# Key copies one group per three steps, the second batch's keys loaded two units later, and two reordered loads in a block-sparse attention plus MoE kernel

## The chip, the core and the metric

The kernel runs on one core of one Trainium2 chip. The metric is device time in microseconds. Three runs of the kernel before gave 733.57 us in the median (733.33 to 733.93).

## What is computed

Block-sparse attention over 4 batches, 8 heads, 768 positions and head size 64, then a two-layer network over all 3072 rows. A block of 32 queries sees the blocks next to it, the first and the last block, and three drawn blocks; the first and the last block of queries see everything.

```python
def reference(q, k, v, sampled_blocks, w_in, w_out):
    scores = (q @ k.transpose(0, 1, 3, 2)) / 8            # 4 x 8 x 768 x 768
    mask = (abs(blk_i - blk_j) <= 1) | edge(blk_i) | edge(blk_j)   # edge: block 0 or 23
    for qb in range(24):
        for kb in sampled_blocks[qb]:                     # three drawn per block of queries
            mask[32*qb:32*qb+32, 32*kb:32*kb+32] = True
    attn = softmax(where(mask, scores, -1e9))
    x = (attn @ v).transpose(0, 2, 1, 3).reshape(3072, 512)
    h = maximum(x @ w_in, 0)                              # w_in 512 x 2048
    return (h * h) @ w_out                                # w_out 2048 x 512
```

## The kernel before, in words

**Tiles and halves.** A tile is 128 positions of one batch, so there are 24, numbered k = 0 to 23 over (batch b, tile t), six to a batch. A tile is worked in two halves u, four heads each (class Half, L423). One half makes the scores on TensorE (L481, tile `s_t_u`), maxima on VectorE (L493), exponentials on ScalarE, a transpose, and the product with the values on TensorE (L576, tile `pv_t_u`). The two whole query blocks of a batch are a unit of their own kind (class Whole, L627, score tile `g`).

**Gathered keys.** The scores of a tile read a buffer KG, in which the keys that each group j of 32 queries needs lie side by side: two fixed blocks, three drawn ones and three neighbours. Two buffers, `KG_84` and `KG_85` in the order tool's names, take turns, and a third serves tile 2 alone. For tiles 0 to 6 GpSimd fills KG out of the batch's natural keys `kn` (one tile for each half, loaded whole by `load_keys`, L185). `copy_keys` (L284) is a generator: for each half it makes the window copies (L317, three instructions) and, for the first tiles of a batch, the fixed blocks (L352), and then for each group j three copies (L299) with a `yield` behind them. So one group per call of `next`. A tile has 4 groups a half, or 3 where an edge block is left out (tiles 0 and 5 of a batch). From tile 7 on KG is loaded by DMA (`load_kg`, L333).

**The network.** Rows go through it in chunks c of three tiles. In chunk 0 the weights are still being prepared: every 128-wide slice f of either layer is loaded as a raw 64-bit tile by a DMA that GpSimd issues (`craw`, L832), cut by ScalarE (L848, L850) and assembled by VectorE (L859, L860) into `W` (first layer) or `WO` (second). A first-layer slice is then split (`split`, L898) into a high part, cast by ScalarE (L901), and a low part, a subtraction on GpSimd (L904); both are the tile `wi_f`. TensorE multiplies three times: high by high, high by low and low by high (L939, tile `ph_f`), so its third matmul of a slice needs GpSimd's subtraction. The second layer is L983 (chunk 0) and L993 (later), tile `po`. The raw tiles and `wi` share one rotating set of seven buffers.

**What sets the order.** Every engine works through its own list in the order in which the code issues instructions; the five lists wait for each other by semaphores. First comes a start phase (L1115 to L1142) with the attention of chunk 0. Then `moe(c)` is a generator whose every `yield` is a step `now` (L1153). In each step of chunk 0 the loop first calls `more_keys` (L328; it advances the oldest unfinished `copy_keys` by one group), then cuts and loads weights, and then lets the units of chunk 1 (tiles 3 to 5) and chunk 2 go on (`work.step`). The halves of tiles 3, 4 and 5 start in steps 4, 16, 28, 40, 52 and 64 (STEP_1 and FIRST_1), those of tile 6, the first of the second batch, in steps 67 and 83. The split of slice f + 1 is issued where slice f begins, about every sixth step.

**Loads of the second batch.** `Half.loads` (L598) with step 0 runs right behind a half's scores. In tile 4 of the first batch (t = NT - 2) it calls `load_keys` for the next batch on GpSimd's DMA queue; in tile 5 it adds the whole blocks' queries and the values `vn`, also there. The drawn rows of values (L396) and the fixed ones (L211, L215) go by SyncE's queue.

**`prepare`** (L1087) runs once, in step 8 of the start phase: the rest of tile 1's keys, its windows of values, drawn rows for tile 1, then for tile 2 (the third tile) the fixed value blocks (`load_static`), the drawn rows and four groups of keys, with one raw-weight load (`advance("load")`) among them.

Of the kernel before, what the change touches and what calls it, by code (L numbers as in the profile page):

```python
# [18 lines left out]
SP = mybir.EngineType.SP  # L19
# [3 lines left out]
B, H, S, D = 4, 8, 768, 64  # L23
# [4 lines left out]
NT = S // P  # L28
NJ = P // BLK
# [52 lines left out]
SOON = 12  # L82
SPLIT_1 = 4
BITS_1 = 5
STEADY = 11
V_3 = (4, 9)

KEYS_0 = 8
# [18 lines left out]
def tile_block_sparse_attention_moe(ctx: ExitStack, tc, kd, knd, qd, qgd, vd, vnd, samp, const, wcat, out):  # L107
# [9 lines left out]
    nc = tc.nc  # L117
# [63 lines left out]
    def load_whole(b, eng=nc.sync):  # L181

        eng.dma_start(QG.rearrange("p a b -> p (a b)"), qgd[b])

    def load_keys(b, u, eng=nc.sync):  # L185

        kn = rot.tile([P, NBLK, 2, BLK], F32, tag=f"kn{u}", name=f"kn{b}_{u}", bufs=1)
        eng.dma_start(kn.rearrange("p a b c -> p (a b c)"), knd[b, u])
        st["kn", b, u] = kn

    def values_of(k):

        return V[k if k < UC else 0]
# [4 lines left out]
    def halves(k, u):  # L198

        if k < UC:  # L200
            return slice(0, 2) if u == k // 2 else None
        return slice(u, u + 1)

    def columns(src, us):

        return src.rearrange("... (u c) -> ... u c", u=2)[..., us, :]

    def load_static(k, u, eng=nc.sync, j=0, n=1):
        if k < UC:
            src = vd[order[k][0], V_STATIC * BLK :].unsqueeze(1).broadcast_to([2 * BLK, n, HW])  # L210
            eng.dma_start(VJ[k][0][0 : 2 * BLK, j : j + n], src)  # L211
            return
        src = columns(vd[order[k][0], V_STATIC * BLK :], u)
        src = src.unsqueeze(1).broadcast_to([2 * BLK, NJ, HW // 2])
        eng.dma_start(values_of(k)[0][0 : 2 * BLK, u], src)  # L215
# [7 lines left out]
    def place(k, j, n):  # L223

        return (j + n - 1 if 0 < k < UC else 1 + n) % NJ
# [19 lines left out]
    def load_vn(b, hf, eng=nc.sync, own=None):  # L245

        vn = (own or rot).tile([P, NT, HW // 2], F32, tag="vn", name=f"vn{b}_{hf}", bufs=1)
        eng.dma_start(vn.rearrange("p t c -> p (t c)"), vnd[b, hf])
        st["vn", b, hf] = vn

    def groups(t):

        return tuple(range(1 if t == 0 else 0, NJ - 1 if t == NT - 1 else NJ))
# [4 lines left out]
    def sampled(t, i, on):  # L258
        n = NJ * NRAND
        a = (2 * t + i) * n  # L260
        return nc.values_load_multi_w_load_instructions(
            st["idx"][0:1, a : a + n],
            engines=[on],
            min_val=0,
            max_val=NBLK - 2,
            skip_runtime_bounds_check_because="products of a block's index with 0 or 1, that is zero unless the index is 1 to 22",
        )[1]

    def load_q(b, t, eng=nc.sync, own=None):
        q = (own or rot).tile([P, NJ, NPAIR, BLK], F32, tag="q", name=f"q{b}_{t}", bufs=1 if own else 2)  # L270
        n = NJ * NPAIR * BLK
        eng.dma_start(q.rearrange("p a b c -> p (a b c)"), qd[b, :, t * n : (t + 1) * n])
        st["q", b, t] = q

    def keys_of(b, t, own=None):

        k = order.index((b, t))
        st["kg", b, t] = own.tile([P, NJ, NK, NPAIR, BLK], F32, name=f"KG{k}") if own else KG[(k - (k >= UC)) % 2]
# [5 lines left out]
    def copy_keys(b, t):  # L284

        vals = sampled(t, 0, POOL)
        k, kg = order.index((b, t)), st["kg", b, t]
        for u in range(2):
            copy = nc.gpsimd.tensor_copy
            if t < UC:  # L290
                static_keys(b, t, u, copy)
            if 0 < k < UC:
                key_edges(k, u, copy)
            else:
                key_windows(k, u, copy)
            kn = st["kn", b, u]
            for j in groups(t):
                for r in range(NRAND):
                    copy(  # L299
                        kg[:, j, key_place(k, j, r), 2 * u : 2 * u + 2].unsqueeze(1),  # L300
                        kn[:, bass.ds(vals[NRAND * j + r], 1)],
                    )
                yield
# [71 lines left out]
    def load_sampled(k, u, eng, on, which=range(NRAND), js=None):  # L375
        us = halves(k, u)
        if us is None:
            return
        b, t = order[k]
        VA, VB = values_of(k)  # L380
        if (b, t) not in drawn:
            drawn.clear()
            drawn[b, t] = sampled(t, 1, on)
        vals = drawn[b, t]
        if k < UC:
            v4 = vd[b].rearrange("(a p) c -> p a c", p=BLK)
        else:
            v4 = columns(vd[b], us).rearrange("(a p) u c -> p a u c", p=BLK)
        for j in sorted(groups(t)) if js is None else js:
            for r in which:  # L390
                a = (place(k, j, 3) if r == 2 else 2 + r) * BLK
                if k < UC:
                    dst = VJ[k][r == 2][a : a + BLK, j]
                else:
                    dst = (VB if r == 2 else VA)[a : a + BLK, us, j]
                eng.dma_start(dst.unsqueeze(1), v4[:, bass.ds(vals[NRAND * j + r], 1)])  # L396
# [26 lines left out]
    class Half:  # L423
# [174 lines left out]
        def loads(self, step):  # L598

            k = order.index((self.b, self.t))  # L600
            eng = nc.gpsimd if self.b == 0 else nc.sync
            if step == 0 and self.t == NT - 2 and self.b + 1 < B:
                load_keys(self.b + 1, self.u, eng)
            if step == 0 and self.t == NT - 1 and self.b + 1 < B:
                if self.u == 0:
                    load_whole(self.b + 1, eng)
                    load_vn(self.b + 1, 0, eng)
            n = k + (UC if k < UC - 1 else UC - 1)
            if step == 0 and self.u == 1 and k != UC - 1 and n < len(order):
                if k < UC:  # L610
                    held.append(order[n])
                else:
                    load_q(*order[n])
                if n <= 2 * UC:
                    keys_of(*order[n])
                    if n < 2 * UC:
                        later.append(copy_keys(*order[n]))
                elif self.moved:
                    load_kg(*order[n])
            if step == 0 and self.u == 0 and k == 2 * UC - 1:  # L620
                later.append(copy_keys(*order[k + 1]))
            if step == 1 and self.u == 1 and 2 * UC < n < len(order):
                load_kg(*order[n])
            if step == 2 and k >= UC and k + 1 < len(order):
                load_values(k + 1, self.u, self.t == NT - 1)
# [251 lines left out]
    def advance(stage):  # L877

        if done[stage] < len(cuts):
            stages[stage](*cuts[done[stage]])  # L880
        done[stage] += 1
# [205 lines left out]
    def prepare():  # L1087
        key_windows(1, 1, nc.gpsimd.tensor_copy)
        deque(keys[1], 0)
        for f in windows(1, 0) + windows(1, 1):  # L1090
            f(nc.gpsimd.tensor_copy)
        load_sampled(1, 0, nc.sync, SP, (2,))
        load_static(2, 1, n=NJ)
        load_sampled(2, 1, nc.sync, SP, (0, 1))
        for j in groups(2):
            next(keys[2])
            if j == 1:
                advance("load")

    def rest(i):  # L1100
        if i == 0:
# [22 lines left out]
    now = 0  # L1124
# [25 lines left out]
    now = 0  # L1150
    for c in range(NCH + 1):
        work.drain(c, now)
        for _ in moe(c):  # L1153
            now += 1
            if c or now > SPLIT_1 and (now < STEADY or now % 2 == 0):
                more_keys()
            if c == 0 and now == SPLIT_1:
                wi1[0, 2] = split(0, W1[2], "wi0_2")
            if c == 0 and now == V_3[0]:
                nc.gpsimd.memset(V[0][1][BLK : BLK + 1, 0, 0, 0:1], 0.0)  # L1160
            if c == 0 and now in V_3:
                load_window(UC, V_3.index(now))
                load_sampled(UC, V_3.index(now), nc.sync, SP)
                if held:
                    load_q(*held.pop())
            if c == 0 and now == BITS_1:
                advance("bits")
            soon = now in CUT_1 or now >= SOON and now % 3 == 0
            if c == 0 and soon and done["split"] < len(cuts):
                cut_next()  # L1170
            if now < begins(c + 1) - LAST:
                work.step(now)
            else:
                work.step(now)
                work.drain(c + 1, now)
# [58 lines left out]
```

## Time and profile before

| | |
|---|---|
| median of three runs | 733.57 us |
| the profiled execution | 734.13 us, of which 732.2 us are its span |
| granted TensorE clock, mean | 0.999 |
| TensorE matmul busy | 707.3 us (97%) |
| GpSimd busy | 555.0 us (76%) |
| VectorE busy | 533.2 us (73%) |
| ScalarE busy | 501.3 us (68%) |

The profile is one execution, with times in us from the span's start. Rows of its timeline give start, length, engine, line, operation, output and input tile and a count, and in square brackets how long the engine had been idle before and what ended the wait. PE is TensorE, PEld its weight loads, DVE VectorE, ACT ScalarE, POOL GpSimd, SP SyncE; a q behind a name is that engine's DMA queue. A row "PE busy (x)" of a table by stretches gives us busy and a count of instructions.

### The profile page before, as it was taken

To read this page: it belongs to the slowest core of one execution; us is meant where nothing else is said; L and a number is where in the kernel's file an instruction comes from. 1 tells how busy PE (TensorE), PEld (TensorE's weight loads), DVE (VectorE), ACT (ScalarE), POOL (GpSimd) and SP (SyncE) were. 2 spreads that over 40 slices of the span, in tenths; PEclk is the share of its full clock that TensorE was granted. 3 is DMA by queue.
4 is the path that set the end of the run, shared out by engine and by line. 5 is a ranking of instruction groups with operands and counts; after the bars stand their busy time and mean duration, and the time that the engine had idled before them with its cause. 6 is when DMAs were issued, how large, how long until landed. Compare 5 with 4: busy or idle time off the path is not lost.

```text
span 732.2 us, 21483 instructions
## 1 busy us (share of the span) xinstructions
PE 707.3 (97%) x7496; PEld 565.7 (77%) x7496; DVE 533.2 (73%) x1056; ACT 501.3 (68%) x1118; POOL 555.0 (76%) x711
## 2 busy tenths in 40 slices
PE   5889999999999999999999999999999999999997
PEld 2666666677788888777878888887778888888996
DVE  5787889687686868678776877768777686647552
ACT  5888787998757856688866875678776767622222
POOL 8979977368766768869786687768877577868985
PEclk9999999999999999999999999999999999999999
DMA  8869999655554565564635556635455352101001
GB/s 272 195 203 289 281 342 238 156 152 135 165 137 113 170 200 145 119 162 112 182 87 139 161 161 188 155 91 150 129 139 148 96 154 51 34 1 44 1 1 43
DMA packets 91934, 105.10 MB, mean 144 GB/s; under 512 B 13715, under 2 KB 77716, under 8 KB 91828
## 3 DMA queue, kind: packets, MB, share of 16 engines
q1 hardware_dynamic: 86020, 81.15, 41.7%
q0 software_dynamic: 5664, 22.45, 9.4%
q8 instruction: 60, 0.98, 0.6%
q14 instruction: 46, 0.38, 0.2%
q10 hardware_dynamic: 144, 0.13, 0.1%
HBM read 97.39 MB, written 6.29 MB: 142 GB/s over the span
## 4 chain that ended last, share of the span: by engine, by line
PE 65%; DVE 12%; ACT 6%; POOL 6%; DMA 4%; issue 3%; SPq 2%; POOLq 0%; DVEq 0%; ACTq 0%
PE ph L939 27%; PE po L993 25%; PE pv L576 5%; PE s L481 5%; DVE m L493 2%; POOL KG L299 2%; PE po L983 1%; DMA craw<-in_w_dram 1%; DVE p L500 1%; DVE pT L531 1%; SPq L396 1%; DVE xl L927 1%; DMA vn<-in_vn_dram 1%; DMA V<-in_v_dram 1%; ACT pm L525 1%
## 5 line engine op out<-in xcount | busy, mean ns | idle before, releaser
L939 PE MATMUL ph<-xh,wi 128*128 128x384 f32 x960 | 275.4, 347 | 0.6 <-POOL wi L904 0.6
L525 ACT ACTIVATE pm<-p 32x256 f32<-32x256 f32 x528 | 219.2, 415 | 15.6 <-DVE p L500 8.4
L993 PE MATMUL po<-wo,gh 128*128 128x512 f32 x672 | 211.7, 396 | 0.0
L904 POOL TENSOR_TENSOR wi<-W,wi 128x512 fp32r<-128x512 f32 x120 | 164.0, 1366 | 56.8 <-DVE wi L903 29.5
L939 PEld LDWEIGHTS ph<-xh,wi 128*128 128x128 f32 x960 | 173.9, 188 | 23.6 <-issue 11.6
L960 ACT ACTIVATE r<-ph 128x384 f32<-128x384 f32 x128 | 62.9, 492 | 170.1 <-PE ph L939 169.4
L904 POOL TENSOR_TENSOR wo<-WO,wo 128x512 fp32r<-128x512 f32 x112 | 144.6, 1291 | 34.1 <-DVE wo L903 32.7
L973 POOL TENSOR_TENSOR gl<-gf,gh 128x384 fp32r<-128x384 f32 x112 | 118.7, 1060 | 64.8 <-DVE gf L971 55.6
L939 PE MATMUL ph<-xl,wi 128*128 128x384 f32 x480 | 161.9, 337 | 0.0
L993 PEld LDWEIGHTS po<-wo,gh 128*128 128x128 f32 x672 | 123.0, 188 | 26.9 <-issue 7.5
L971 DVE SCALAR_TENSOR_TENSOR gf<-ph,r 128x384 f32<-128x384 f32 x112 | 62.0, 554 | 107.5 <-ACT r L960 99.5
L993 PE MATMUL po<-wo,gl 128*128 128x512 f32 x336 | 134.7, 401 | 5.3 <-POOL gl L973 4.9
L939 PEld LDWEIGHTS ph<-xl,wi 128*128 128x128 f32 x480 | 90.2, 188 | 8.9 <-issue 5.2
L903 DVE CAST wo<-WO 128x512 fp32r<-128x512 f32 x112 | 86.3, 770 | 0.0
L993 PEld LDWEIGHTS po<-wo,gl 128*128 128x128 f32 x336 | 63.0, 187 | 25.8 <-POOL gl L973 12.6
L966 ACT ACTIVATE gh<-r 128x384 fp32r<-128x384 f32 x112 | 58.9, 526 | 10.1
L493 DVE TENSOR_REDUCE m<-s 128x2 f32<-128x512 f32 (+1 forms) x96 | 61.1, 676 | 1.7 <-PE s L481 1.7
L903 DVE CAST wi<-W 128x512 fp32r<-128x512 f32 x105 | 61.3, 583 | 0.0
L576 PEld LDWEIGHTS pv<-V,pT 128*32 128x32 f32 x2816 | 42.8, 110 | 23.2 <-issue 10.4
L576 PE MATMUL pv<-V,pT 128*32 128x65 f32 x2816 | 51.4, 222 | 4.8 <-ACT pT L565 3.8
L481 PE MATMUL s<-KG,q 64*32 64x256 f32 x1408 | 53.8, 382 | 0.2 <-ACT r L960 0.2
L983 PE MATMUL po<-WO,gp 128*128 128x512 f32 x96 | 46.8, 602 | 0.0
(94 smaller groups left out, 775.4 us busy)
## 6 DMA issues: line engine op xcount, KB each, us to landing
craw<-in_w_dram POOLq DMA_DIRECT2D x32, 512.0 KB, 5.6
V<-in_v_dram SPq DMA_DIRECT2D x462, 32.5 KB, 2.5
KG<-in_k_dram SPq DMA_DIRECT2D x189, 64.0 KB, 1.9
V<-in_v_dram SPq DMA_DIRECT2D x28, 390.0 KB, 4.9
KG<-in_k_dram SPq DMA_DIRECT2D x12, 768.0 KB, 5.7
q<-in_q_dram SPq DMA_DIRECT2D x24, 256.0 KB, 3.1
out_dram<-ot SPq DMA_DIRECT2D x23, 256.0 KB, 5.7
V<-in_v_dram SPq DMA_DIRECT2D x14, 292.5 KB, 5.6
```

The costliest lines, as they stand in the source:

```text
L481: nc.tensor.matmul(self.sb[e][g * BLK : (g + 1) * BLK, i * NSLOT : (i + 1) * NSLOT], q[r, j, pr, :], kg[r, j, :, pr, :], start=True, stop= ...
L493: nc.vector.tensor_reduce(m[at, e], self.sb[e][at].rearrange("p (i c) -> p i c", i=2), axis=AX, op=ALU.max)
L525: nc.scalar.activation(p[a * BLK : (a + 1) * BLK, g], x[g * BLK : (g + 1) * BLK, :, a], AF.Exp, scale=SCALE)
L576: nc.tensor.matmul(po[h * BLK : (h + 1) * BLK, g * VW : (g + 1) * VW], self.pT[:, g, 2 * e + i, c], v[:, self.u, j, h * VW : (h + 1) * VW] ...
L903: nc.vector.tensor_copy(w[:, 0], src)
L904: nc.gpsimd.tensor_tensor(w[:, 1], src, w[:, 0], op=ALU.subtract)
L939: nc.tensor.matmul(ph[c, f][:, :TOK], wi[:, w, cc], x[:, cc], start=(cc == 0 and i == 0), stop=(cc == NCC - 1 and i == 2),)
L960: nc.scalar.activation(r, acc[:, :TOK], AF.Relu)
L966: nc.scalar.activation(gh, r, AF.Square)
L971: nc.vector.scalar_tensor_tensor(gf, acc[:, :TOK], 0.0, r, op0=ALU.max, op1=ALU.mult)
L973: nc.gpsimd.tensor_tensor(gl, gf, gh, op=ALU.subtract)
L993: nc.tensor.matmul(acc[c][u], g[:, at], w[:, k], start=(f == 0 and i == 0), stop=(f == NF - 1 and i == 2))
```

## The change

Three things change, and the constant STEADY goes.

- In chunk 0 `more_keys` was called in every step from 5 to 10 and in every second step from 12 on. Now it is called in steps 5, 8, 11, 14 and so on.
- For the second batch `load_keys` is called from tile 5 (t = NT - 1), two units later, and is issued by SyncE. For the third and fourth batch it stays where it was.
- In `prepare` the raw-weight load comes ahead of everything of tiles 1 and 2 that follows, the drawn rows of tile 2 are issued group by group between the key copies, and its fixed value blocks come behind the rows of three groups.

```diff
-STEADY = 11
...
-            if step == 0 and self.t == NT - 2 and self.b + 1 < B:
-                load_keys(self.b + 1, self.u, eng)
+            if step == 0 and self.t == NT - (2 if self.b else 1) and self.b + 1 < B:
+                load_keys(self.b + 1, self.u, nc.sync)
...
+        advance("load")
         load_sampled(1, 0, nc.sync, SP, (2,))
-        load_static(2, 1, n=NJ)
-        load_sampled(2, 1, nc.sync, SP, (0, 1))
         for j in groups(2):
+            if j == NJ - 1:
+                load_static(2, 1, n=NJ)
+            load_sampled(2, 1, nc.sync, SP, (0, 1), (j,))
             next(keys[2])
-            if j == 1:
-                advance("load")
...
-            if c or now > SPLIT_1 and (now < STEADY or now % 2 == 0):
+            if c or now > SPLIT_1 and now % 3 == 2:
                 more_keys()
```

The lists of TensorE, VectorE and ScalarE keep their order, instruction by instruction; GpSimd's and SyncE's change. (Line numbers behind L82 are one lower in the changed kernel.)

GpSimd's list in the first steps of chunk 0, before. `KG_84` is filled for tile 3 here and `KG_85` for tile 4; `wi_3` and `wi_4` are the splits of slices 3 and 4.

```order
L317 COPY KG_84<-kn_1_128 128x4x64 x3
...
L832 DMA craw_0_1317<-in_w_dram 128x1024
L904 TENSOR_TENSOR wi_3_1321<-W_82,wi_3_1321 128x512
...
L299 COPY KG_84<-kn_1_128 128x64
L261 TENSOR_LOAD idx
L317 COPY KG_85<-kn_0_120 128x4x64 x3
...
L832 DMA craw_1_1422<-in_w_dram 128x1024
L904 TENSOR_TENSOR wi_4_1424<-W_83,wi_4_1424 128x512
```

The same stretch in the changed kernel:

```order
L316 COPY KG_84<-kn_1_128 128x4x64 x3
...
L831 DMA craw_0_1314<-in_w_dram 128x1024
L903 TENSOR_TENSOR wi_3_1318<-W_82,wi_3_1318 128x512
...
L831 DMA craw_1_1382<-in_w_dram 128x1024
L903 TENSOR_TENSOR wi_4_1384<-W_83,wi_4_1384 128x512
L298 ISA
L298 COPY KG_84<-kn_1_128 128x64
...
L260 TENSOR_LOAD idx
L316 COPY KG_85<-kn_0_120 128x4x64 x3
```

Before, all four groups of tile 3's second half stand ahead of the split `wi_4`, with three groups of tile 4 between. Now the fourth group stands behind `wi_4`, and tile 4's first window copies behind that. In the same way the last group of tile 4's two halves now stands behind `wi_6` and `wi_8`, and that of tile 6's first half behind `wi_12`.

TensorE's list at the scores of tile 3's second half and at slice 4, before, with the engines that each instruction waits for in brackets:

```order
L939 MATMUL ph_3_1452<-xh_737,wi_3_1321 128x384
L481 MATMUL s_3_1_0_1463<-KG_84,q_3_779 32x256 [waits DVE_49]
L481 MATMUL s_3_1_1_1464<-KG_84,q_3_779 32x256 [waits Activation_49]
...
L481 MATMUL s_3_1_0_1463<-KG_84,q_3_779 32x256 [waits Pool_49]
...
L939 MATMUL ph_4_1606<-xh_737,wi_4_1424 128x384 [waits PE_49]
L939 MATMUL ph_4_1606<-xl_738,wi_4_1424 128x384
L939 MATMUL ph_4_1606<-xh_737,wi_4_1424 128x384 [waits Pool_49]
```

And in the changed kernel, where the row with a wait for Pool stands three times among the scores (groups 1, 2 and 3):

```order
L938 MATMUL ph_3_1412<-xh_737,wi_3_1318 128x384
L480 MATMUL s_3_1_0_1417<-KG_84,q_3_779 32x256 [waits DVE_49]
L480 MATMUL s_3_1_1_1418<-KG_84,q_3_779 32x256 [waits Activation_49]
L480 MATMUL s_3_1_0_1417<-KG_84,q_3_779 32x256 [waits Pool_49]
...
L938 MATMUL ph_4_1588<-xh_737,wi_4_1384 128x384 [waits PE_49]
L938 MATMUL ph_4_1588<-xl_738,wi_4_1384 128x384
L938 MATMUL ph_4_1588<-xh_737,wi_4_1384 128x384 x2
```

No matmul moved. The wait for GpSimd that slice 4's third matmul had is gone, because a score matmul ahead of it in TensorE's list now waits for a GpSimd instruction that stands behind `wi_4`.

SyncE's list at the loads of tile 5's values, before (`V` are the values, `q_1` the queries of tile 7):

```order
L396 DMA V_79<-in_v_dram 32x260
L370 DMA V_79<-in_v_dram 96x3x260
...
L396 DMA V_79<-in_v_dram 32x260
L272 DMA q_1_2287<-in_q_dram 128x512
L215 DMA V_78<-in_v_dram 64x4x260
```

And in the changed kernel, with `kn_0` and `kn_1` the second batch's keys for either half:

```order
L395 DMA V_79<-in_v_dram 32x260
L187 DMA kn_0_2068<-in_kn_dram 128x1536
L369 DMA V_79<-in_v_dram 96x3x260
...
L395 DMA V_79<-in_v_dram 32x260
L187 DMA kn_1_2269<-in_kn_dram 128x1536
L271 DMA q_1_2271<-in_q_dram 128x512
L214 DMA V_78<-in_v_dram 64x4x260
```

Each key load now stands in SyncE's queue behind the drawn rows of one half of tile 5, and ahead of the next load of that queue.

## The prediction

> **What bounds the kernel now.** I read the page's head and its busy shares first, then a table by stretches, then TensorE's waits in the stages that the change touches, and then the timeline row by row.
>
> ```profile
> span 732.2 us, 21483 instructions
> PE 707.3 (97%) x7496; PEld 565.7 (77%) x7496; DVE 533.2 (73%) x1056; ACT 501.3 (68%) x1118; POOL 555.0 (76%) x711
> ```
>
> TensorE is busy for 97% of the span, so a change that moves no matmul can only move the end by the 24.9 us in which TensorE is idle, or add to them. Where these lie is in the table by stretches. Its columns are the stretch, its length, and the busy time of PE, PEld, DVE, ACT and POOL with instructions in brackets, then the granted clock, the DMA share and GB/s.
>
> ```profile
> 60.00:70.00 10.00, 9.50 (x121) 5.86 (x120) 9.26 (x10) 8.90 (x16) 9.98 (x23) 1.00 0.88 260
> 80.00:90.00 10.00, 8.93 (x106) 6.18 (x113) 8.88 (x11) 8.53 (x18) 9.56 (x20) 1.00 0.97 277
> ...
> 190.00:200.00 10.00, 8.21 (x117) 6.53 (x115) 5.21 (x11) 8.35 (x20) 8.23 (x11) 1.00 0.74 225
> 200.00:220.00 20.00, 20.00 (x243) 16.85 (x232) 16.40 (x38) 11.02 (x25) 13.63 (x12) 1.00 0.51 138
> ```
>
> From 60 to 70 GpSimd is busy for 9.98 of 10 us, and TensorE for 9.50. This is the stage in which GpSimd copies keys and splits weights at once. The waits of TensorE from 45 to 200 us, with the sum, the number and the longest:
>
> ```profile
> PE po L993 <- POOL gl L973: 1.1, 1, 1.1
> PE pv L576 <- ACT pT L565: 0.8, 3, 0.4
> PE pvg L740 <- DMA vn<-in_vn_dram: 0.6, 1, 0.6
> PE ph L939 <- POOL wi L904: 0.6, 1, 0.6
> PE s L481 <- ACT r L960: 0.2, 1, 0.2
> ```
>
> So in all the stretch only one wait of 0.6 us is for the splits, and none for copied keys. Copies that are spread out more can win back little here. What they can lose is larger, and that is the argument below. A measurement of this kernel can tell about 0.2%, 1.5 us, from no change.
>
> **The calls of every third step: a new wait at the scores of tile 3's second half.** The four groups of that half are now copied in steps 5, 8, 11 and 14, the scores stand in step 16, and the fourth group has come to stand behind the split `wi_4` in GpSimd's list. That split needs ScalarE's cast of slice 4.
>
> ```profile
> 62.17 1.09 PE L481 MATMUL s<-KG,q 64*32 64x256 f32 x30 [0.24 <-ACT r L960]
> ...
> 63.15 0.78 ACT L850 ACTIVATE craw<-craw,below 128x512 int32<-128x512 uint16 x1
> 64.29 0.62 ACT L901 CAST wi<-W 128x512 fp32r<-128x512 f32 x1 [0.36 <-DVE W L860]
> ...
> 66.26 0.58 POOL L299 COPY KG<-kn 128x64 f32 x3
> ...
> 67.33 1.28 POOL L904 TENSOR_TENSOR wi<-W,wi 128x512 fp32r<-128x512 f32 x1
> 68.55 1.52 POOL L299 COPY KG<-kn 128x64 f32 x3
> ```
>
> The cast starts at 64.29 and ends at 64.91. GpSimd split behind it only at 67.33, since copies stood ahead; in the new order these are gone, and I let the split start at 64.91. It takes 1.28, to 66.19. Then come three copies, 0.58 at best and 1.52 where they were slowed: 66.8 to 67.7. The first score matmul of the fourth group is the 7th of 16 in the order (each a pair in the profile), so TensorE reaches it some 6/16 of 1.09 into the row at 62.17, at 62.6. The wait is 4.2 to 5.1 us. Could the cast come sooner? It waited 0.36 for VectorE; ahead of that ScalarE was occupied until 63.93, by cuts that no moved instruction releases. So the lower bound is 4.2 − 0.36 = 3.8. I take **+4.3**, near the unslowed copies, since VectorE has work of its own to wait for then: its maxima need these scores. Nothing hides the wait: TensorE's list is strict, and pv, ph and po of the same steps stand behind the scores.
>
> **What that takes away.** While TensorE stands, the others catch up. The waits that follow within a few steps are these, with ScalarE's cause of the second:
>
> ```profile
> 67.15 1.18 PE L576 MATMUL pv<-V,pT 128*32 128x65 f32 x62 [0.19 <-ACT pT L565]
> 80.50 1.14 PE L576 MATMUL pv<-V,pT 128*32 128x65 f32 x64 [0.44 <-ACT pT L565]
> 89.20 0.62 PE L939 MATMUL ph<-xh,wi 128*128 128x384 f32 x2 [0.63 <-POOL wi L904]
> ...
> 78.66 0.67 ACT L848 ACTIVATE W<-craw 128x512 f32<-128x512 f32 x1 [1.52 <-DMA craw<-in_w_dram]
> ```
>
> The 0.44 comes from a raw load that ScalarE awaited 1.52 us; with TensorE over 4 us later it is there in time. The 0.63 is for a split that stood behind copies, which now stand behind it. I take all three, 0.19 + 0.44 + 0.63 = **−1.3**; at the least the 0.63 alone goes.
>
> **The same order twice more.** The last group of tile 4's halves stands behind `wi_6` and `wi_8`. Whether a score waits there depends on the time from the end of a first-layer slice, whose result ScalarE must take before it casts the next, to the scores. No row shows that order yet; the nearest one for ScalarE's part is a later slice, and the ends of two slices and the scores behind them stand below it.
>
> ```profile
> 111.03 0.49 ACT L960 ACTIVATE r<-ph 128x384 f32<-128x384 f32 x1 [0.17 <-PE ph L939]
> 113.21 0.63 ACT L901 CAST wi<-W 128x512 fp32r<-128x512 f32 x1
> ...
> 71.33 1.88 PE L983 MATMUL po<-WO,gp 128*128 128x512 f32 x4
> 75.65 1.09 PE L481 MATMUL s<-KG,q 64*32 64x256 f32 x32
> ...
> 84.61 1.88 PE L983 MATMUL po<-WO,gp 128*128 128x512 f32 x4
> 89.76 1.09 PE L481 MATMUL s<-KG,q 64*32 64x256 f32 x32
> ```
>
> From r to the end of the cast it is 113.21 + 0.63 − 111.03 = 2.81; with the split's 1.28 and copies of 0.58 to 1.52 the keys are there 4.7 to 5.6 after the slice. TensorE needs them 75.65 + 0.4 − 71.33 = 4.7 after it in the first place, and 89.76 + 0.4 − 84.61 less the 0.63 that goes = 4.9 in the second. That makes waits of 0 to 0.9 and of 0 to 0.7. I take **+0.6** for both, since slowed and quick copies are about as frequent; the bounds are 0 and 1.6.
>
> **The raw load in `prepare`.** It now stands ahead of the key copies of tile 2.
>
> ```profile
> 25.68 0.53 POOL L832 DMA_DIRECT2D craw<-in_w_dram  x1
> ...
> 31.29 0.81 ACT L848 ACTIVATE ct<-craw 128x512 f32<-128x512 f32 x1 [0.74 <-DMA craw<-in_w_dram]
> ...
> 35.66 0.42 PE L576 MATMUL pv<-V,pT 128*32 128x65 f32 x12 [0.94 <-issue]
> ```
>
> It is issued about 2 us sooner, and ScalarE's 0.74 for it goes. Whether TensorE has the good of it is open, because a gap of 0.94 with no releaser comes before 35.66. From 0 to −0.74; I take the middle, **−0.4**. The fixed value blocks and the drawn rows that change places on SyncE are not awaited before the stall in any row, and I cost them at nothing; their cover is the stretch to tile 2's product, and if it failed, the price would be part of the 0.94.
>
> **The second batch's keys.** They leave GpSimd's queue, two issues of 0.53 in stretches where no wait hangs on GpSimd, so nothing. On SyncE the first half's load stands behind nine drawn rows. Its rows, with the size and the median time to landing of the two queues:
>
> ```profile
> 96.37 9.90 SPq L396 DMA_DIRECT2D V<-in_v_dram  x9
> ...
> kn<-in_kn_dram POOLq DMA_DIRECT2D x4, 768.0 KB, 7.9
> kn<-in_kn_dram SPq DMA_DIRECT2D x4, 768.0 KB, 4.3
> ...
> 106.35 1.17 POOL L352 COPY KG<-kn 128x512 f32<-128x512 f32 x1 [0.38 <-issue]
> ...
> 115.12 0.60 POOL L352 COPY KG<-kn 128x512 f32<-128x512 f32 x1
> ...
> 118.36 1.08 PE L481 MATMUL s<-KG,q 64*32 64x256 f32 x24
> ```
>
> The rows end at 96.37 + 9.90 = 106.27; the keys land 4.3 to 7.9 later, at 110.6 to 114.2. The copies of tile 6's first half ran from 106.35 to 115.12 before, 8.8 us with the splits among them. That gives 119.4 to 123.0, where TensorE needs the last group at 118.36 + 0.5 = 118.9 in the old times and at 122.1 if it runs 3.2 later. I cost it at nothing in the main case: the cover is TensorE's delay. Without it the price is below, as a rival. The later values, the drawn rows and the waits of 1.1 and 0.6 behind 190 us have feeders that move with TensorE; 0, with 0.6 either way.
>
> The sum is 4.3 − 1.3 + 0.6 − 0.4 = +3.2. The profiled execution took 734.13, of which the span is 732.2; it becomes 737.3 with a span of 735.4. The median of three is 0.56 under the profiled one, so I forecast 733.57 + 3.2 = **736.8 us**. The bounds together are 3.8 − 1.3 + 0 − 0.7 − 0.6 = +1.2 and 5.1 − 0.6 + 1.6 + 0.6 = +6.7.
>
> **The rivals.** *TensorE's clock falls in the new wait.* Four idle us are longer than any but the opening's.
>
> ```profile
> 6.67 2.84 PE L670 MATMUL g<-kn,QG 64*64 64x384 f32 x16 [6.67 <-DMA kn<-in_kn_dram]
> ...
> 12.74 1.56 PE L670 MATMUL g<-kn,QG 64*64 64x384 f32 x8 [0.36 <-DMA kn<-in_kn_dram]
> ...
> 16.04 0.88 PE L670 MATMUL g<-kn,QG 64*64 64x384 f32 x8
> ```
>
> After 6.67 idle us, sixteen matmuls took 2.84 where twice 0.88 is the later rate, and the next eight 1.56: 1.08 + 0.68 = 1.8 us lost. If the wait of 4.3 does the same, the time is 736.8 + 1.8 = 738.6. For it: the wait is two thirds of the opening's. Against it: the opening is a first start, no other idle stretch of four us stands in the trace, and in the table above the granted clock is 1.00 in all stretches. I give 0.20. [...]
>
> *The second batch's keys come late.* With the landing of 7.9, tile 6's scores get their last group at 123.0 against 118.9, a wait of 4.1 less what TensorE runs late; with the middle of the landings 2.3 on top of the sum: 739.1. It decides where SyncE's drawn rows move with TensorE as well. For it, GpSimd's queue took 7.9 for this load; against it, SyncE's took 4.3, and TensorE's delay hides up to 3.2. I give 0.10.
>
> *The wait is made up.* At its lower bound of 3.8, with 1.3 and 0.7 won, no loops and up to another 1.0 of the waits behind 190 us: 3.8 − 1.3 − 0.7 − 1.0 = +0.8, 734.4. The dense stretch from 200 speaks for it only weakly; I give 0.12.
>
> *Faster.* The one mechanism is that slice 4's cast comes 4.3 us or more sooner, before 60.6, because raw tiles arrive sooner and the chain of cuts moves up with them. Then the new wait is gone, and the early load and the three waits give −0.7 − 1.3 = −2.0: 731.6. Against it, ScalarE's row at 63.15 stands right before the cast and the cut it follows is not released by GpSimd's copies. I give 0.08.
>
> **How the numbers follow.** The main case has 0.50, with a range of its own from 735.4 to 738.6. The clock has 0.20, the late keys 0.10, the wait made up 0.12, and the faster case 0.08. The range of 734.6 to 739.6 takes in the first three and half of the fourth; left out are the faster case and the rest of the fourth, and the ends of the late keys. Within 1.5 us of 733.57 lies most of the wait made up and a little of the main case, 0.14; faster 0.08; slower the rest, 0.78.
>
> **What would show it.** In the changed profile: a wait for GpSimd's key copies of 3.8 to 5.1 us in TensorE's row of scores near 62 us, with the split `wi` ending just before the copies that end it; the row at 89 without its 0.63; scores near 80 and 93 with under 1 us each; ScalarE without a wait near 31. Matmuls behind the new wait at 0.88 for eight of the 64x384 kind, or at half that rate, tell the clock. The forecast is wrong if that wait is under 2 us, or if a wait on kn of over 1 us stands ahead of tile 6's scores.

## The result and the profile after

The changed kernel took 739.87 us in the median of four runs (739.11 to 741.86), where the kernel before took 733.45 (733.17 to 733.93). The ratio is 1.0091 (95% interval 1.0069 to 1.0113): slower by 6.4 us, and 0.27 us beyond the upper end of the forecast range. The page of the changed kernel begins:

```profile
span 738.3 us, 21479 instructions
PE 711.0 (96%) x7496; PEld 567.9 (77%) x7496; DVE 526.8 (71%) x1056; ACT 500.4 (68%) x1118; POOL 553.8 (75%) x709
```

The same 7496 matmuls are busy for 711.0 us instead of 707.3, so 3.7 of the 6.1 us of added span are not waits at all: the matmuls themselves were longer. Among TensorE's waits over the whole span there is one row that the kernel before did not have (us in total, number, longest):

```profile
PE s L480 <- POOL KG L298: 5.4, 4, 3.9
```

The longest of the four is the one that the prediction worked out. The timeline around it, first TensorE, then ScalarE and GpSimd:

```profile
61.14 0.67 PE L480 MATMUL s<-KG,q 64*32 64x256 f32 x10 [0.24 <-ACT r L959]
65.75 1.92 PE L480 MATMUL s<-KG,q 64*32 64x256 f32 x20 [3.93 <-POOL KG L298]
...
62.74 0.60 ACT L900 CAST wi<-W 128x512 fp32r<-128x512 f32 x1
...
63.42 1.28 POOL L903 TENSOR_TENSOR wi<-W,wi 128x512 fp32r<-128x512 f32 x1 [1.19 <-ACT wi L900]
64.64 1.05 POOL L298 COPY KG<-kn 128x64 f32 x3
```

GpSimd stood 1.19 us for the cast, made the split and copied the fourth group; that copy ends at 64.64 + 1.05 = 65.69, and TensorE goes on at 65.75. The stretches behind that, with the granted clock as the third number from the end:

```profile
63.00:64.00 1.00, 0.00 (x0) 0.00 (x0) 0.97 (x2) 1.00 (x3) 0.57 (x1) 1.00 1.04 300
64.00:65.00 1.00, 0.00 (x0) 0.00 (x0) 1.00 (x1) 1.00 (x3) 1.00 (x2) 0.92 1.02 309
65.00:66.00 1.00, 0.25 (x8) 0.23 (x16) 0.25 (x1) 0.50 (x2) 1.00 (x4) 0.50 1.15 243
...
69.00:70.00 1.00, 1.00 (x4) 1.00 (x4) 0.96 (x2) 0.00 (x0) 0.00 (x0) 0.50 1.07 294
...
71.00:72.00 1.00, 1.00 (x3) 0.48 (x2) 0.00 (x0) 0.97 (x3) 0.49 (x1) 0.66 0.44 100
72.00:73.00 1.00, 1.00 (x15) 0.24 (x17) 0.16 (x1) 1.00 (x3) 0.00 (x0) 1.00 0.63 181
```

The granted clock went to one half (0.50) near the end of the wait and stayed there until some 71.7 us. Twenty score matmuls took 1.92 us there; groups of twenty later took 1.05, as the next rows show. They are the later scores that wait, and the second layer's matmuls that mark the places; the row that stands alone behind them is of the kernel before.

```profile
76.92 1.88 PE L982 MATMUL po<-WO,gp 128*128 128x512 f32 x4
...
82.32 1.05 PE L480 MATMUL s<-KG,q 64*32 64x256 f32 x20 [0.50 <-POOL KG L298]
...
90.70 1.88 PE L982 MATMUL po<-WO,gp 128*128 128x512 f32 x4
...
96.10 1.05 PE L480 MATMUL s<-KG,q 64*32 64x256 f32 x20 [0.50 <-POOL KG L298]
...
124.69 1.23 PE L480 MATMUL s<-KG,q 64*32 64x256 f32 x8
126.41 1.05 PE L480 MATMUL s<-KG,q 64*32 64x256 f32 x16 [0.49 <-POOL KG L298]
127.40 1.13 PE L982 MATMUL po<-WO,gp 128*128 128x512 f32 x2
```

```profile
119.37 1.13 PE L983 MATMUL po<-WO,gp 128*128 128x512 f32 x2
```

Matched row by row with those of before, TensorE was 1.03 us ahead at the scores of tile 3 (62.17 and 61.14). It was 5.59 behind at 76.92 (71.33 before), 6.09 at 90.70 (84.61), 6.33 at 124.69 (118.36) and 8.03 at 127.40 (119.37). At the end it was 6.1 behind, by the spans. So:

| term | forecast | here | from |
|---|---|---|---|
| early loads | −0.4 | −1.0 | 61.14 against 62.17 |
| wait at tile 3's second half | +4.3 | +3.9 | its row |
| clock behind it | only as a rival, +1.8 | +2.7 | 5.59 + 1.03 − 3.93, less what went at 67 |
| waits that went at 80 and 89 | −1.1 of the 1.3 | −1.1 | no such wait is left |
| tile 4's two waits | +0.6 | +1.8 | (6.09 − 5.59 + 0.44) + (6.33 − 6.09 + 0.63) |
| tile 6's wait | 0, rival +2.3 | +1.7 | 8.03 − 6.33 |
| behind 127 us | 0 | −1.9 | 6.1 − 8.03 |
| sum | +3.2 | +6.1 | |

Of the 1.9 won at the end, 0.6 is the wait for `vn` near 197, which is gone; the rest lies in short steps that no row names. The wait at tile 6 is the surprise. GpSimd's rows ahead of the scores of its first half, and the first one for its second half:

```profile
117.53 0.94 POOL L351 COPY KG<-kn 128x512 f32<-128x512 f32 x1 [0.35 <-issue]
...
121.88 1.29 POOL L903 TENSOR_TENSOR wi<-W,wi 128x512 fp32r<-128x512 f32 x1
123.11 2.13 POOL L298 COPY KG<-kn 128x64 f32 x3
...
125.78 0.58 POOL L298 COPY KG<-kn 128x64 f32 x3
...
130.55 0.61 POOL L351 COPY KG<-kn 128x512 f32<-128x512 f32 x1 [2.42 <-DMA kn<-in_kn_dram]
```

GpSimd did not wait for the new keys of the first half: its first copy of them came after 0.35 of "issue". From there to 126.36 it worked without a gap, with the split `wi_12` ahead of the last two groups and slowed copies of 2.13 behind it. So the late group stands behind a split, as at tiles 3 and 4, but this split did not wait for its cast, and how much of the 0.49 is the split's is not separated. For the second half's keys GpSimd did stand 2.42; no wait of TensorE followed from it.

### The profile page after: what moved, and what is told of

Read it like the earlier page. It is cut to its first block, busy times and chain, and to the rows that moved or that the text cites. A ratio compares the mean times of both kernels' runs of the same rounds, so it can differ in the third digit from the quotient of the medians.

```text
span 738.3 us, 21479 instructions
## 1 busy us (share of the span) xinstructions
PE 711.0 (96%) x7496; PEld 567.9 (77%) x7496; DVE 526.8 (71%) x1056; ACT 500.4 (68%) x1118; POOL 553.8 (75%) x709
## 4 chain that ended last, share of the span: by engine, by line
PE 77%; DVE 8%; POOL 6%; issue 5%; ACT 3%; DMA 1%; POOLq 0%; DVEq 0%; ACTq 0%
PE ph L938 31%; PE po L992 27%; PE s L480 6%; PE pv L575 5%; PE po L982 3%; POOL KG L298 2%; PE pvg L739 2%; PE g L669 2%; DVE m L492 1%; POOL gl L972 1%; DVE p L499 1%; DVE pT L530 1%; DVE gf L970 1%; PE pt L554 1%; POOL pgm L705 1%
## 5 line engine op out<-in xcount | busy, mean ns | idle before, releaser
L902 DVE CAST wo<-WO 128x512 fp32r<-128x512 f32 x112 | 84.6, 755 | 0.0
L480 PE MATMUL s<-KG,q 64*32 64x256 f32 x1408 | 57.7, 386 | 5.7 <-POOL KG L298 5.4
```

What stands on the lines that cost most here:

```text
L480: nc.tensor.matmul(self.sb[e][g * BLK : (g + 1) * BLK, i * NSLOT : (i + 1) * NSLOT], q[r, j, pr, :], kg[r, j, :, pr, :], start=True, stop= ...
L902: nc.vector.tensor_copy(w[:, 0], src)
```

## The experiments

The theory after the result: the loss is made by key copies that stand behind a split in GpSimd's list, at four places, and by TensorE's clock, which fell in the longest of these waits. The rivals: the spread of the copies costs by itself, the late keys on SyncE's queue cost, or what is slow behind the wait has another cause than the clock. Kernels of one group ran on one chip with the kernel before beside them: experiments 1, 2, 3 and 5 are the first group, 4, 6 and 7 the second, 8 and 9 the third. The runs of the kernel before lay at 730.6 to 738.4 us in the first group (median 733.29), 731.8 to 736.4 in the second (733.31) and 730.9 to 737.0 in the third (732.67). Each time below is a median, with the ratio to the kernel before and its 95% interval; the ratio is estimated on its own and need not equal that of the medians.

**1. Prepare alone undone.** In the changed kernel:

```diff
-        advance("load")
         load_sampled(1, 0, nc.sync, SP, (2,))
+        load_static(2, 1, n=NJ)
+        load_sampled(2, 1, nc.sync, SP, (0, 1))
         for j in groups(2):
-            if j == NJ - 1:
-                load_static(2, 1, n=NJ)
-            load_sampled(2, 1, nc.sync, SP, (0, 1), (j,))
             next(keys[2])
+            if j == 1:
+                advance("load")
```

> The changed kernel with the old order in prepare, so that the calls of every third step and the late keys are alone. Theory: the loss lies wholly in the calls; the new order in prepare gained some 0.3 us of the 1.0 that TensorE was ahead at 60 us, the rest being arrival times of the first loads. So 739.9 + 0.3 = 740.2, with the same wait of about 3.9 us near 62 us. Rival: prepare gained the whole 1.0, 740.9.

740.0 us (ratio 1.0072, 1.0044 to 1.0099), with a wait of 3.4 us and a half-clock stretch of 3.41 us. The loss is that of the calls and the late keys together; the late keys alone were not run. Whether prepare is worth 0.1 or 1 us inside the changed kernel can't be told: the two kernels ran in different groups.

**2. Prepare alone done**, the reverse of that diff in the kernel before.

> The kernel before with only the new order in prepare. Theory: 0.3 us gained early and kept, 733.45 - 0.3 = 733.2, no wait for key copies. Rival, as in the prediction's bound, 0.7 to 1.0 gained: 732.5 to 732.8. A third outcome, that a later wait takes it back: 733.5.

732.38 us, ratio 0.9974 (0.9957 to 0.9992): faster, by 0.9 us in the medians of its group. That is the rival's figure, not the theory's 0.3.

**3. The wait filled with work.** In `scores` of the changed kernel, in front of the first matmul of tile 3's fourth group, the score matmuls of groups 0 to 2 are done again, five times over:

```diff
-                for g, j in enumerate(self.js):
+                again = (b, t, u, i) == (0, 3, 1, 0)
+                for g, j in [*enumerate(self.js[:3])] * (5 * again) + [*enumerate(self.js)]:
```

> The changed kernel with 30 score matmuls of groups 0 to 2 of tile 3's second half done again, same inputs and same place, ahead of the first matmul that waits: about 2 us of added work in a wait of 3.9 us. Theory: the clock falls because TensorE stands for 3.9 us; with about 1.9 us of standing left it stays at 1.00, and the kernel with more work is faster by the 2.5 to 3 us lost at half clock: 737.0 to 737.4. Rival: the slow stretch behind the wait has another cause (the refill after a stop, or the dense transfers there), the granted clock falls all the same and the time stays at 739.9.

738.24 us (1.0055, 1.0035 to 1.0075). Its trace, first TensorE's rows, then the stretches behind:

```profile
61.25 3.39 PE L481 MATMUL s<-KG,q 64*32 64x256 f32 x70 [0.24 <-ACT r L960]
65.91 1.05 PE L481 MATMUL s<-KG,q 64*32 64x256 f32 x20 [1.27 <-POOL KG L298]
```

```profile
64.00:65.00 1.00, 0.64 (x13) 0.11 (x2) 1.00 (x1) 1.00 (x3) 1.00 (x2) 1.00 0.97 351
65.00:66.00 1.00, 0.09 (x8) 0.09 (x16) 0.41 (x1) 0.69 (x2) 1.00 (x4) 1.00 0.98 370
66.00:67.00 1.00, 1.00 (x21) 0.43 (x22) 0.01 (x1) 0.00 (x0) 0.65 (x2) 1.00 1.12 290
```

The keys come at the same time, 65.9, but the clock stays at 1.00 and the twenty matmuls behind take 1.05 instead of 1.92, with transfers as dense as before (DMA shares of 0.97 to 1.12). So neither the transfers nor the refill after a stop, of 1.27 us here, made them slow. The time is between the theory's 737.0 to 737.4 and the rival's 739.9, 1.8 under experiment 1 of the same group, which differs by the old order in prepare.

**4. The same with 42 matmuls**, beside the changed kernel on one chip.

> The changed kernel again, unaltered, so that the others of this group stand beside it on one chip: 739.9, in single runs 739.1 to 741.9, the higher ones with a lower mean granted clock.

> As the run with 30 score matmuls done again, but with 42, so that nearly the whole wait of 3.9 us at tile 3's second half is filled. Theory (the clock falls because TensorE stands): no half-clock stretch, 1.6 to 3 us faster than the changed kernel of the same group, though 42 matmuls are added: 737 to 738.3. Rival (what is lost behind the wait is no matter of the clock): the changed kernel's time or more, 739.9 or above.

The changed kernel took 740.47 (1.0094, 1.0076 to 1.0113), the filled one 737.46 (1.0055, 1.0038 to 1.0072). The intervals do not overlap, if barely: 42 added matmuls make the kernel 3.0 us faster. That is what the fallen clock cost in the medians; with 30 matmuls 1.8 were won back, so 3.0 is not exact. The traced run of the filled kernel is its longest, 741.48. TensorE stood in it ahead of the filled place, for exponentials of ScalarE, which had stood 3.28 us for raw weights:

```profile
60.70 1.97 PE L555 MATMUL pt<-ident,p 128*128 128x128 f32 x8 [2.98 <-ACT p L540]
...
69.25 1.05 PE L481 MATMUL s<-KG,q 64*32 64x256 f32 x20 [0.97 <-POOL KG L298]
```

The clock was at one half from 60.0 to 63.4, around that first wait. Behind the filled one it stayed at 1.00.

**5. One call more**, so that every later group comes a call sooner and no last group of tile 3 or 4 stands behind a split.

```diff
-            if c or now > SPLIT_1 and now % 3 == 2:
+            if c or now > SPLIT_1 and (now % 3 == 2 or now == 10):
```

> The changed kernel with one more call of more_keys in step 10, so that every later group comes three steps sooner and the last groups of tile 3's and tile 4's halves stand ahead of the splits again; the spread, the late keys and prepare stay. Theory: the loops through the splits are the whole loss (3.9 wait, about 3 of clock and refill, 1.5 and 1.7 for the three short ones), while the waits that went (0.8 for a split at 89, about 1 early, some behind 160) mostly stay gone: 732 to 733. Rival: the spread or the late keys on SyncE's queue cost something by themselves: 734.5 or more.

736.79 us (1.0022, 0.9996 to 1.0048): by the median the rival's figure of 734.5 or more, though three of the twelve runs, at 732.4 to 732.9, are the theory's; nine lie at 735.1 to 739.1. The interval of the ratio includes 1, so neither slower nor faster is shown. The waits at tile 3 and 4 are gone from its trace; another has come at tile 6. SyncE's issue of the keys, GpSimd's rows and TensorE's, and the stretch with its clock:

```profile
103.16 0.36 SPq L187 DMA_DIRECT2D kn<-in_kn_dram  x1
...
105.19 1.30 POOL L903 TENSOR_TENSOR wi<-W,wi 128x512 fp32r<-128x512 f32 x1 [1.02 <-ACT wi L900]
114.05 0.61 POOL L351 COPY KG<-kn 128x512 f32<-128x512 f32 x1 [7.56 <-DMA kn<-in_kn_dram]
...
117.04 0.62 PE L480 MATMUL s<-KG,q 64*32 64x256 f32 x4 [1.44 <-POOL KG L298]
118.14 0.97 PE L480 MATMUL s<-KG,q 64*32 64x256 f32 x4 [0.48 <-POOL KG L298]
120.41 1.92 PE L480 MATMUL s<-KG,q 64*32 64x256 f32 x16 [1.30 <-POOL KG L298]
```

```profile
118.00:120.00 2.00, 0.97 (x4) 0.14 (x4) 0.00 (x0) 1.22 (x4) 1.99 (x5) 0.57 1.09 382
```

The keys were there 10.9 us after their issue (103.16 to 114.05), later than either queue's median in the prediction (7.9 and 4.3), and GpSimd stood 7.56 for them. So the rival of the late keys is real, but TensorE did not show it in the changed kernel: its copies of the first half came so late themselves that the keys were there.

**6. The keys on GpSimd's queue.** The kernel of 5, with

```diff
-                load_keys(self.b + 1, self.u, nc.sync)
+                load_keys(self.b + 1, self.u, eng)
```

> The kernel with the added call in step 10, and the second batch's keys issued by GpSimd instead of SyncE at the same point of the program, so ahead of the values vn in GpSimd's queue. Theory: what that kernel still lost was GpSimd's wait of 7.6 us for these keys ahead of tile 6's scores; issued at 101.3 instead of 103.2 and landing some 8 us later they are there at 109, GpSimd waits under 3 us, TensorE under 0.5, and no half-clock stretch: 730 to 732. Rival: the transfers of that stage are what is slow, whichever queue: TensorE still waits over 2 us for tile 6's keys, 735 or more.

737.10 us (1.0021, 0.9994 to 1.0048): five runs from 730.6 to 732.4 at a mean clock of 0.997 to 0.999, seven from 737.0 to 739.6 at 0.990 to 0.996. By the median that is the rival's time, but not its mechanism: no score of tile 6 waited. The theory held for the first half, where GpSimd waited 0.90. For the second half GpSimd now issues its load directly ahead of its own copies and waits for all of it, the next split behind:

```profile
108.96 0.61 POOL L351 COPY KG<-kn 128x512 f32<-128x512 f32 x1 [0.90 <-DMA kn<-in_kn_dram]
...
118.22 0.53 POOL L187 DMA_DIRECT2D kn<-in_kn_dram  x1
126.74 0.61 POOL L351 COPY KG<-kn 128x512 f32<-128x512 f32 x1 [8.00 <-DMA kn<-in_kn_dram]
...
132.51 1.01 PE L938 MATMUL ph<-xh,wi 128*128 128x384 f32 x2 [4.08 <-POOL wi L903]
```

A queue was exchanged for a place in a list; the wait moved from the scores to the network's slices, and the clock was at one half from 130.7 to 137.5.

**7. The keys as soon as there is room.** The kernel of 5, with the first half loaded in step 46 by GpSimd, the second half by SyncE as in the change:

```diff
+            if c == 0 and now == 46:
+                load_keys(1, 0, nc.gpsimd)
...
-            if step == 0 and self.t == NT - (2 if self.b else 1) and self.b + 1 < B:
+            if step == 0 and self.t == NT - (2 if self.b else 1) and self.b + 1 < B and (self.b or self.u):
```

> The kernel with the added call in step 10, and the first half of the second batch's keys loaded in step 46 by GpSimd, as soon as the old keys are copied out; the second half as in the changed kernel. Theory: the keys are there before GpSimd comes to them near 106, no wait at tile 6's scores, every loop gone: 730 to 731.5, faster than the kernel before by the waits that the change removed. Rival: the spread of the copies has a price of its own: 733 or more with no wait for key copies in the trace.

730.70 us, ratio 0.9965 (0.9947 to 0.9983): faster than the kernel before, with the gain of prepare (experiment 2) in it. Its traced run, the longest of twelve at 735.2, was slowed early, near 36 us, by a wait of 3.14 us for which its trace names no releaser, and by the clock, which was at one half from 37.3 to 44.1. From 55 to 240 us TensorE's waits are these, and no score waits for copies:

```profile
PE po L992 <- POOL gl L972: 1.4, 2, 1.1
PE s L480 <- ACT r L959: 0.3, 1, 0.3
```

So the spread of the copies has no price of its own that this kernel shows.

**8 and 9. The first place alone, and the later ones alone.** In the changed kernel, the call of step 14 made in step 10:

```diff
-            if c or now > SPLIT_1 and now % 3 == 2:
+            if c or now > SPLIT_1 and now != 14 and (now % 3 == 2 or now == 10):
```

> The changed kernel with the call of step 14 moved to step 10 and nothing else: only tile 3's last group stands ahead of its split again, all later groups stay where the change put them. Theory (each loop has its own price): the 7 us of the wait and its half-clock stretch go and 0.4 to 0.7 of waits on ScalarE at 67 and 80 come back; the three short loops stay: 7 - 0.5 = 6.5 below the changed kernel, 733.4 to 734.0. Rival (the short loops were short only because the long wait let ScalarE and GpSimd catch up): they grow by the same amount, waits for key copies of over 1 us each near 76, 90 and 118, 735 or more.

736.98 us (1.0045, 1.0029 to 1.0061), above the theory's 734 and at the rival's 735 or more; of the rival's three grown waits the trace has one. The waits for copies in its trace, at tile 4's halves and tile 6:

```profile
78.85 1.05 PE L480 MATMUL s<-KG,q 64*32 64x256 f32 x20 [2.15 <-POOL KG L298]
92.63 1.05 PE L480 MATMUL s<-KG,q 64*32 64x256 f32 x20 [0.50 <-POOL KG L298]
122.77 1.05 PE L480 MATMUL s<-KG,q 64*32 64x256 f32 x16 [0.50 <-POOL KG L298]
```

The next wait grew from 0.50 to 2.15. That the long wait had let the other engines catch up is the likely reason, but it is argued. The two behind it kept their size. Part of the 736.98 is not the copies' at all: near 40 us this trace has waits of 0.95 (no releaser named) and of 0.61 and 0.54 for values, and at 67.22 TensorE was 0.56 behind the kernel before, where the changed kernel had been 1.03 ahead at 61. And the other way round, the kernel of 7 with its added call in step 16 instead of 10:

```diff
-            if c or now > SPLIT_1 and (now % 3 == 2 or now == 10):
+            if c or now > SPLIT_1 and (now % 3 == 2 or now == 16):
```

> The changed kernel with one more call in step 16 instead of step 10 and the second batch's first keys loaded in step 46 by GpSimd: tile 3's loop stays, the later ones at tile 4 and tile 6 go. Theory: the three short ones are worth the 0.7 + 0.8 + 1.7 = 3.2 by which the matmuls behind them fell back: 740.2 - 3.2 = 737.0, one wait for key copies near 62 of 3.4 to 3.9 us, with a half-clock stretch behind it. Rival: what the short ones cost is hidden elsewhere anyway, 739 or more.

736.22 us (1.0055, 1.0030 to 1.0081), near the theory's 737.0, with one wait for copies:

```profile
PE s L480 <- POOL KG L298: 3.4, 1, 3.4
```

By the ratios, the change costs 0.94%, with only the later places left 0.45%, with only the first left 0.55%, and with none −0.35% (first and last from the second group, the others from the third). By the medians that is +7.2, +4.3, +3.6 and −2.6 us. Counted from the last of these kernels, the later places cost 6.9, the first 6.2 and both together 9.8: the two do not add up.

## Why the prediction was wrong

*The direction and the mechanism of the new wait were right.* The wait stood where the order put it, was 3.93 us within 3.8 to 5.1, and was ended by the copies behind `wi_4`. The cast stood right behind the cuts; counted from the scores' row it ended 0.5 sooner than before (63.34 − 61.14 against 64.91 − 62.17), the copies took 1.05, between the two bounds, and TensorE reached the fourth group 0.2 later than reckoned. Together that makes 3.93 and not 4.3.

*The step that failed is "The main case has 0.50 ... The clock has 0.20, the late keys 0.10".* The clock was treated as an alternative to the main case and left out of the sum. It is a consequence of it: a wait of the length that I forecast is what made the clock fall. In the four traces with a wait of 3.4 us or more at tile 3 (the change and its repeat, experiments 1 and 9) it fell each time; with the wait filled down to 1.27 (experiment 3) it stayed at 1.00. What was held against it, a clock of 1.00 in all stretches, came from a trace that had no such wait in mid-kernel. Added to the sum, even at the 1.8 of the opening, the clock would have given 738.6, with a range of 736.4 to 741.4 around it.

*The size of the clock's term.* In the changed kernel's trace the clock was at half from 64.85 to 71.68, of which 5.9 us lay behind the wait. Half of that is 3.0, which is also what experiment 4 measured. In the traces of the repeat and of experiments 1 and 9 the stretch was half as long, 3.41 us, worth some 1.7. So the opening's 1.8 fits the short stretch and not the long one. The opening was a doubtful measure all the same: its matmuls were slow, but the granted clock reads 1.00 in every two microseconds from 6 to 20.

*"I take +0.6 for both"* was mis-sized: both waits were 0.50, as the bounds of 0.9 and 0.7 allowed, but each set the following rows back by about 0.9. A stop cost more than its idle time here: the 32 scores of tile 4's halves took 2.13 and 2.14 us up to the next row (81.17 to 83.30, 94.95 to 97.09), where they took 1.02 before. The bound of 1.6 was near the 1.8 of the table.

*"I cost it at nothing in the main case"*, of tile 6: there it cost 1.7. The prediction let the copies begin when the keys land, 4 to 8 us later than before, and last 8.8 us. They did last 126.36 − 117.53 = 8.8, with one split among them as before. But they began 11.2 us later than at 106.35, with the keys there: tile 5's last groups, one per three steps, stood ahead of them until 116.6. The prediction priced the landing and not these calls, nor the place of the last groups behind `wi_12`, which the words on the change name. TensorE was only 6.3 behind. The rival's price of 2.3 was near, its reason wrong for the changed kernel; experiment 5 shows that it stood just behind. The sign "a wait on kn of over 1 us ... ahead of tile 6's scores" came true for the second half, on GpSimd alone.

*The new order in prepare* was priced by the raw load alone, its moved value loads "at nothing". TensorE has a new stop in the product of tile 0's second half:

```profile
30.36 0.67 PE L575 MATMUL pv<-V,pT 128*32 128x65 f32 x33 [1.43 <-issue]
```

All ten traces with the new order have a stop at this place, of 0.45 to 1.94 us; the kernel before and experiment 1 have none. No row names what releases it, so which of the moved loads brings it stays open. Other waits go, since experiment 2 is faster all the same.

*Right:* the waits at 80 and 89 went (−1.1), and ScalarE has no wait near 31. *Too small:* the early loads, 0.4 against 1.0. But 0.7 of this was no gain of prepare: the second whole-block scores began at 12.02 instead of 12.74, and GpSimd's first moved instruction stands at 23.29. That leaves 0.3 for prepare, near the forecast. Too small as well were the waits behind 190, where I took 0 and the end gained 1.9.

*Luck:* the bounds added together, +1.2 to +6.7, hold the measured +6.3 from 733.57, but with neither the clock nor tile 6's wait in them. The misses of the clock, tile 4 and tile 6 add to 5.6, and 2.5 of that was taken back by the early loads and the end.

## What to carry to other kernels

Where a helper engine's list is thinned out, look for the last piece of each job and what now stands ahead of it: a piece that comes behind an instruction which itself follows the bottleneck's latest result turns into a wait of the whole loop, 3.93 us at tile 3 here. When a forecast contains a wait like the seven of 2.98 to 4.08 us that these traces show on TensorE behind the opening, the clock's price belongs in the sum and not among the rivals: each of the seven had a half-clock stretch of 3.41 or 6.83 us beside it. And waits in a row are not simply added up: in experiments 8 and 9 the two parts alone cost 6.9 and 6.2 us where the whole cost 9.8.

## What the runs showed of the hardware

In the twelve traces, up to their last two microseconds, the granted clock fell to one half nine times, for 3.41 us (five times) or 6.83 us (four times). These lengths come from its means over stretches of 0.1 us. Waits of 3.4 to 3.9 us at tile 3 and of 4.08 in experiment 6 stood before or around five of the falls.

Shorter waits had a fall beside them too: 2.98 us in experiment 4, 3.14 in experiment 7, and in experiment 6 one of 1.94, whose clock was at half from 31.7 to 35.1. A wait of 2.15 (experiment 8) and one of 1.27 (experiment 3) left it at 1.00.

```profile
30.89 0.67 PE L575 MATMUL pv<-V,pT 128*32 128x65 f32 x33 [1.94 <-issue]
```

In experiment 5 no wait in mid-kernel was longer than 1.44 us. The clock fell at 118.3, behind waits of 1.44 and 0.48 with a few matmuls between, and before the third one, of 1.30. So the length of one gap does not decide it in these traces. In the 3.41 us ahead of the nine falls TensorE was busy for 0.05 to 1.49 us. How little that is does not decide it alone either: the 3.41 us around the wait of 2.15 hold 1.26 busy us, and the clock did not fall. What decides stays open.

The mean granted clock of the changed kernel's four runs was 0.998 at 739.11, 0.994 at 739.34, 0.995 at 740.40 and 0.993 at 741.86. By estimate from the lengths above, one stretch of 3.41 us at half makes a mean of 0.998 over 738 us, and one of 6.83 makes 0.995.

A load of 768 KB took 4.3 us to landing on SyncE's queue and 7.9 on GpSimd's, by the medians in the kernel before. In experiment 5 it was 10.9 from its issue to the end of GpSimd's wait for it; values, a raw load of 512 KB and drawn rows were issued between 1.4 us ahead of it and 2.2 behind.
